# K of the first 48 units transposed on TensorE as pairs of bf16 in 4-byte elements

## The chip, the cores and the metric

One core of a Trainium2 chip. The metric is the device time of one execution in microseconds. "The profile" of a kernel is one profiled execution of it.

A word on names. The kernel works through 512 **units** (32 batches of 16 heads; 256 units belong to problem A, then 256 to problem B). One **step** of its schedule handles one unit on each engine, each engine being some units ahead of or behind the others. PE is TensorE, PEld its weight loads, DVE is VectorE, ACT is ScalarE, POOL is GpSimd.

## The reference, cut to what matters

Two independent problems with the same shapes, outputs side by side:

```python
B, Sq, D = 16, 144, 448          # x: B x Sq x D
H, Sk, Dh = 16, 512, 256         # k_cache, v_cache: B x H x Sk x Dh
q = (x @ wq).reshape(B, Sq, H, Dh).transpose(0, 2, 1, 3)
scores = einsum("bhqd,bhkd->bhqk", q, k_cache) * Dh ** -0.5
p = softmax(scores, axis=-1)
o = einsum("bhqk,bhkd->bhqd", p, v_cache)
return o.transpose(0, 2, 1, 3).reshape(B, Sq, H * Dh) @ wo
```

Everything is bf16. The scores matmuls of both kernels take K with its 256 columns d on the partitions (`lhsT` in `t_s` below), and so K has to be transposed. The scores that these inputs give are so small that a wrong K still passes the comparison with the reference. So "correct" says little about K here; that the changed kernel pairs the right columns is argued from its indices, not shown.

## The kernel before

K of units 48 to 511 is transposed by the DMA on its way in, 16 units at a time. K of the first 48 units (`P0 = 48`) is loaded as it lies, two units a load, into the same buffers as V, and is transposed on TensorE. Partition p holds keys 4p to 4p+3, 256 columns each, as one row of 1024 bf16.

```python
tr_ps = (s_ps[2][:, :].bitcast(BF16), qp_ps[:, 1, :].bitcast(BF16))   # two PSUM banks
ident = qt_sb[:, NQT - 1, 0, 0:128]                                   # bf16 identity

def t_tr(U, k):                       # half k (0, 1) of unit U; cut
    bank, eng = (("s2", DVE), ("qp1", ACT))[k]
    def e(t):
        for c in range(4):
            a = (4 * k + c) * 128
            ins = t.transpose(tr_ps[k][:, c * 128:(c + 1) * 128], v_sb[:, sl, j, a:a + 128], ident)
        return ins
    S.add(PE, e, ...)
    def ev(g):                        # eviction: DVE for half 0, ACT for half 1
        dst = kt_sb[:, 4 * k:4 * k + 4, ko:ko + 128]
        src = tr_ps[k][:, 0:512].rearrange("p (c q) -> p c q", c=4)
        ...

def t_q(U):                           # Q of one unit: 8 matmuls of 144 columns
    for dc in range(2):
        for kc in range(4):
            c0 = h * DH + dc * 128
            ins = t.matmul(acc, lhsT=wq_sb[:, kc, c0:c0 + 128], rhs=xt_sb[...], ...)

def t_s(U):                           # scores: 8 matmuls of 144 columns, in two banks
    ins = t.matmul(s_ps[bank][:, ...], lhsT=kt_sb[:, 2 * c + dc, ko:ko + 128], rhs=qt_sb[:, qsl, dc, :], ...)
```

In `t.transpose(out, in, ident)` the data are the stationary operand (the weight load), and the identity is the one that moves: 128 columns a transpose. (The records of the run with half the moving columns, below, show it: 64 rows of 128 columns as weight load 64x128, the 64x64 identity in the matmul.)

The order within one step i decides what each engine does first, because an engine takes its instructions in this order, as PE's timeline below shows from 55.13 to 57.08 us (cut to the first 48 units):

```python
t_tr(i + 4, 0)                    # PE: transposes, half 0;  DVE: K eviction
t_q(i + 3); t_evac_q(i + 3)       # PE: Q;                   DVE: Q eviction
t_s(i + 2)                        # PE: scores;              ACT: two exponentials
t_tr(i + 4, 1)                    # PE: transposes, half 1;  ACT: K eviction
t_pv(i); t_sum(i)                 # PE: P times V, sum
t_presum(i + 2)                   # POOL
t_ln(i); t_recip(i)               # ACT: reciprocal of the sum
t_check(i); t_evac_ot(i)          # DVE: two checks of the sum, output eviction
```

## Time and profile before

| | before |
|---|---|
| median of 3 runs | 1057.1 us (1055.59 to 1058.32) |
| profiled span | 1055.3 us |
| PE busy | 98% |
| units 12 to 28 (start of PV to start of PV) | 32.15 us, 2.01 us a unit |
| units 28 to 48 (output projection added) | 51.71 us |
| units 240 to 320 (change from A to B) | 171.06 us |

The stretches are from the start of one unit's first PV matmul to that of another in the profile.

The page of the kernel before: the span, the busy line, and the chain of waits by engine.

```profile
span 1055.3 us, 32320 instructions
...
PE 1031.0 (98%) x12376; PEld 875.0 (83%) x12376; DVE 740.9 (70%) x2039; ACT 793.9 (75%) x2365; POOL 636.6 (60%) x1030
...
PE 91%; DMA 5%; ACT 1%; DVE 1%; SPq 1%; issue 0%; POOL 0%; ACTq 0%; DVEq 0%
```

TensorE is busy nearly all the time, and most of the chain runs through it. "Busy" counts matmuls that overlap in the records (below, a block of eight Q matmuls is recorded as 0.66 us, and the next block starts 0.50 us after it), and so the step has to be read from starts. This is the timeline of PE in the first stage (start us, duration us, engine, line, operation, output and inputs, shape, count):

```profile
55.07 0.23 PE L1158 MATMUL ot_ps<-ps_sb,ones 128*128 128x144 bf16 x1
55.13 0.39 PE L1000 MATMUL s_ps<-qt_sb,v_sb 128*128 128x128 bf16 x4
55.35 0.66 PE L1052 MATMUL qp_ps<-xt_sb,wq_sb 128*128 128x144 bf16 x8
55.85 0.66 PE L1086 MATMUL s_ps<-qt_sb,kt_sb 128*128 128x144 bf16 x8
56.35 0.39 PE L1000 MATMUL qp_ps<-qt_sb,v_sb 128*128 128x128 bf16 x4
56.58 0.66 PE L1142 MATMUL ot_ps<-pt_sb,v_sb 128*128 128x144 bf16 x8
57.08 0.23 PE L1158 MATMUL ot_ps<-ps_sb,ones 128*128 128x144 bf16 x1
```

A block of eight Q matmuls takes 0.50 us from its start to the next block's, 62.5 ns each. Four bf16 transposes take 0.22 us, 56 ns each (the trace has starts to the nanosecond). There is no gap. From one sum matmul to the next it is 2.01 us.

Weight loads of the same stretch (20 to 110 us), by group (busy us, mean ns of one, idle before):

```profile
L1052 PEld LDWEIGHTS qp_ps<-xt_sb,wq_sb 128*128 128x128 bf16 x320 | 20.4, 98 | 0.0
L1000 PEld LDWEIGHTS s_ps<-qt_sb,v_sb 128*128 128x128 bf16 x160 | 11.3, 98 | 4.1 <-DVE run_sb L1209 1.0 <-DVE qt_sb L1065 0.7
```

PE's longest waits on loads other than those at the start (total us, times, longest us):

```profile
PE qp_ps L1052 <- DMA wq_sb<-in_B_wq_dram: 3.6, 1, 3.6
PE s_ps L1086 <- DMA kt_sb<-in_B_k_cache_dram: 2.9, 1, 2.9
```

Both stand between units 240 and 320, where problem A gives way to problem B (at 527 and at 602 us).

### The profile page before, as it was taken

The numbers are of one execution on the slowest core, as the hardware profiler recorded it, in microseconds if no ns is written. First come the engines' busy times: TensorE is split into PE (matmuls) and PEld (weight loads), VectorE is DVE, ScalarE is ACT, GpSimd is POOL, SyncE is SP. The second block draws the span as 40 slices with busy tenths as digits, with TensorE's granted clock in tenths as the row PEclk, the third lists the DMA queues.
The fourth block names the chain that finished last, engine by engine and source line by source line (L and its number), as shares of the span: only waits on it lengthen the run. The fifth ranks groups of instructions, "written<-read, shape, count | busy, mean of one in ns | idle before, by whom it ended". The sixth has DMA issues, their size and how long they took to land.

```text
span 1055.3 us, 32320 instructions
## 1 busy us (share of the span) xinstructions
PE 1031.0 (98%) x12376; PEld 875.0 (83%) x12376; DVE 740.9 (70%) x2039; ACT 793.9 (75%) x2365; POOL 636.6 (60%) x1030
## 2 busy tenths in 40 slices
PE   6999999999999999999999899999999999999997
PEld 6999888888888888888878788888888888888885
DVE  4776666776766777777868667677776667777775
ACT  4887667777777777878857667777877777788785
POOL 3554556656666566666746556566666666666673
PEclk9999999999999999999999999999999999999999
DMA  9999999999999999999999999999999999999960
GB/s 316 372 343 291 294 291 248 283 299 271 264 305 260 248 286 262 304 289 280 283 281 343 279 283 287 303 284 292 251 279 280 278 286 298 296 254 274 292 201 14
DMA packets 589060, 294.15 MB, mean 279 GB/s; under 512 B 500832, under 2 KB 513632, under 8 KB 588896
## 3 DMA queue, kind: packets, MB, share of 16 engines
q1 hardware_dynamic: 588896, 291.99, 110.9%
q8 instruction: 99, 1.62, 0.6%
q14 instruction: 65, 0.53, 0.2%
HBM read 161.48 MB, written 4.13 MB: 157 GB/s over the span
## 4 chain that ended last, share of the span: by engine, by line
PE 91%; DMA 5%; ACT 1%; DVE 1%; SPq 1%; issue 0%; POOL 0%; ACTq 0%; DVEq 0%
PE s_ps L1086 23%; PE ot_ps L1142 23%; PE qp_ps L1052 22%; PE op_ps L1259 19%; DMA kt_sb<-in_B_k_cache_dram 2%; DMA v_sb<-in_A_k_cache_dram 2%; PE ot_ps L1158 2%; PE s_ps L1000 1%; PE qp_ps L1000 1%; DMA wq_sb<-in_B_wq_dram 1%; PE qp_ps L1259 1%; ACT rinv_sb L1179 0%; ACT pt_sb L1096 0%; DVE ring L1194 0%; DVE qt_sb L1066 0%
## 5 line engine op out<-in xcount | busy, mean ns | idle before, releaser
L1106 POOL TENSOR_TENSOR pp_sb<-pt_sb 128x288 f32<-128x288 bf16 x512 | 384.9, 752 | 322.5 <-ACT pt_sb L1096 308.1
L1096 ACT ACTIVATE pt_sb<-s_ps 128x288 bf16<-128x288 f32 x1024 | 364.6, 408 | 184.4 <-PE s_ps L1086 177.6
L1194 DVE TENSOR_TENSOR ring<-ot_ps,rinv_sb 128x288 bf16<-128x288 f32 (+2 forms) x640 | 241.9, 394 | 150.3 <-ACT rinv_sb L1179 145.8
L1086 PE MATMUL s_ps<-qt_sb,kt_sb 128*128 128x144 bf16 x4096 | 341.3, 226 | 4.7 <-DMA kt_sb<-in_B_k_cache_dram 2.9
L1142 PE MATMUL ot_ps<-pt_sb,v_sb 128*128 128x144 bf16 x4096 | 340.3, 226 | 0.0
L1086 PEld LDWEIGHTS s_ps<-qt_sb,kt_sb 128*128 128x128 bf16 x4096 | 287.7, 98 | 56.9 <-DVE qt_sb L1066 5.6
L1179 ACT ACTIVATE rinv_sb<-ln_sb 64x144 f32<-64x144 f32 x928 | 298.3, 321 | 24.3
L1052 PE MATMUL qp_ps<-xt_sb,wq_sb 128*128 128x288 bf16 (+1 forms) x2368 | 302.3, 271 | 6.6 <-DMA wq_sb<-in_B_wq_dram 3.6
L1259 PE MATMUL op_ps<-wo_sb,ring 128*128 128x448 bf16 x1120 | 285.2, 353 | 0.0
L1052 PEld LDWEIGHTS qp_ps<-xt_sb,wq_sb 128*128 128x128 bf16 x2368 | 212.3, 98 | 81.9 <-issue 7.5
L1142 PEld LDWEIGHTS ot_ps<-pt_sb,v_sb 128*128 128x128 bf16 x4096 | 274.5, 98 | 0.5
L1111 POOL TENSOR_TENSOR p_sb<-pp_sb 128x144 f32<-128x144 f32 x464 | 227.5, 490 | 74.6 <-DVE ps_sb L1120 10.4
L1209 DVE TENSOR_REDUCE run_sb<-ot_ps 128x1 bf16<-128x144 f32 x560 | 146.5, 304 | 79.4 <-ACT ln_sb L1166 44.3
L1120 DVE TENSOR_TENSOR ps_sb<-p_sb 64x144 bf16<-64x144 f32 x464 | 158.7, 342 | 44.4 <-POOL p_sb L1111 30.3
L1066 DVE CAST qt_sb<-qp_ps 128x576 bf16<-128x576 f32 x216 | 162.1, 751 | 21.3 <-PE qp_ps L1052 17.7
L1259 PEld LDWEIGHTS op_ps<-wo_sb,ring 128*128 128x128 bf16 x1120 | 94.0, 98 | 21.2
L1166 ACT ACTIVATE ln_sb<-ot_ps 128x144 f32<-128x144 f32 x232 | 67.9, 293 | 32.6 <-PE ot_ps L1158 25.3
L1158 PE MATMUL ot_ps<-ps_sb,ones 128*128 128x144 bf16 x280 | 63.4, 226 | 0.0
L1065 DVE CAST qt_sb<-qp_ps 128x288 bf16<-128x288 f32 x80 | 35.9, 448 | 4.8 <-PE qp_ps L1052 4.3
L1008 ACT ACTIVATE kt_sb<-qp_ps 128x512 bf16<-128x512 bf16 x48 | 28.9, 603 | 7.3 <-PE qp_ps L1000 7.3
L1111 POOL TENSOR_TENSOR ps_sb<-pp_sb 128x144 bf16<-128x144 f32 x48 | 23.5, 490 | 6.9 <-PE ot_ps L1158 0.3
L1158 PEld LDWEIGHTS ot_ps<-ps_sb,ones 128*128 128x128 bf16 x280 | 27.5, 98 | 0.0
(29 smaller groups left out, 153.4 us busy)
## 6 DMA issues: line engine op xcount, KB each, us to landing
v_sb<-in_A_v_cache_dram SPq DMA_DIRECT2D x128, 512.0 KB, 7.1
v_sb<-in_B_v_cache_dram SPq DMA_DIRECT2D x128, 512.0 KB, 7.5
v_sb<-in_A_k_cache_dram SPq DMA_DIRECT2D x24, 512.0 KB, 9.6
out_dram<-ost_sb SPq DMA_DIRECT2D x36, 112.0 KB, 6.2
wo_sb<-in_A_wo_dram SPq DMA_DIRECT2D x8, 448.0 KB, 8.7
wo_sb<-in_B_wo_dram SPq DMA_DIRECT2D x8, 448.0 KB, 9.0
wq_sb<-in_A_wq_dram SPq DMA_DIRECT2D x4, 768.0 KB, 10.1
wq_sb<-in_B_wq_dram SPq DMA_DIRECT2D x4, 768.0 KB, 10.6
```

The source lines that it names most:

```text
L1052: ins = t.matmul(acc, lhsT=wq_sb[:, kc, c0:c0 + 128], rhs=xt_sb[:, kc, xo:xe + 1:max(xe - xo, 1), :], start=(kc == 0), stop=(kc == 3))
L1066: return v.tensor_copy(qt_sb[:, a:b + 1:b - a, :, :], qp_ps[:, :, 0:2 * SQ].rearrange("p e (u q) -> p u e q", u=2))
L1086: ins = t.matmul(s_ps[bank][:, (c % 2) * SQ:(c % 2 + 1) * SQ], lhsT=kt_sb[:, 2 * c + dc, ko:ko + 128], rhs=qt_sb[:, qsl, dc, :], start=(dc ...
L1096: return a.activation(pt_sb[:, psl, 2 * k:2 * k + 2, :].rearrange("p b q -> p (b q)"), s_ps[bank][:, 0:2 * SQ], AF.Exp, scale=DH ** -0.5)
L1106: return g.tensor_tensor(pp_sb[:, :, :], pt_sb[:, psl, 0:2, :], pt_sb[:, psl, 2:4, :], op=ALU.add)
L1111: return g.tensor_tensor(dst, pp_sb[:, 0, :], pp_sb[:, 1, :], op=ALU.add)
L1120: return v.tensor_tensor(ps_sb[p0:p0 + 64, sl, :], p2_sb[0:64, :], p2_sb[64:128, :], op=ALU.add)
L1142: ins = t.matmul(ot_ps[ob][:, dc * SQ:(dc + 1) * SQ], lhsT=v_sb[:, vsl, j, c * DH + dc * 128:c * DH + (dc + 1) * 128], rhs=pt_sb[:, sl, c, ...
L1179: return a.activation(rinv_sb[p0:p0 + 64, sl, :], ln_sb[h0:h0 + 64, :], AF.Exp, scale=-1.0)
L1194: ins = v.tensor_tensor(ring[:, 2 * h:2 * h + 2, r0:r0 + q1 - q0], ot_ps[ob][:, 0:2 * SQ].rearrange("p (c q) -> p c q", c=2)[:, :, q0:q1], ...
L1209: return v.tensor_reduce(run_sb[:, k, j:j + 1], ot_ps[ob][:, 2 * SQ:3 * SQ], axis=AX.X, op=op)
L1259: ins = t.matmul(acc[0:m, 0:D], lhsT=ring[:, c, col0:col0 + m], rhs=wo_sb[:, c, :], start=(c == first), stop=(c == last))
```

## The change

Its intent: two neighbouring bf16 are one 4-byte element. Transposed as such, half as many transposes move the same data (192 and not 384 in the profiles). A row of the result then holds, for a pair of columns d = 2j, 2j+1, both values of each key next to each other. Scores take every second bf16 of it as weights, and Q of these units must pair up in the same way, so it takes `wq` columns in steps of two.

```diff
-        tr_ps = (s_ps[2][:, :].bitcast(BF16), qp_ps[:, 1, :].bitcast(BF16))
-        ident = qt_sb[:, NQT - 1, 0, 0:128]
+        tr_ps = (s_ps[2][:, :], qp_ps[:, 1, :])
+        ident = qt_sb[:, NQT - 1, :, :].rearrange("p e q -> p (e q)").bitcast(F32)[:, 0:128]
...      (a second memset for ones of 4 bytes, from which ident is made)
+        def k_nat(U):
+            c0 = U // KW % (KR // KW) * KW * 128 + U % 2 * 1024
+            return kt_sb[:, U % KW // 2, c0:c0 + 1024]
...
-                for c in range(4):
-                    a = (4 * k + c) * 128
-                    ins = t.transpose(tr_ps[k][:, c * 128:(c + 1) * 128], v_sb[:, sl, j, a:a + 128], ident)
+                for c in range(2):
+                    a = (2 * k + c) * 256
+                    ins = t.transpose(tr_ps[k][:, c * 128:(c + 1) * 128], v_sb[:, sl, j, a:a + 256].bitcast(F32), ident)
...
-                dst = kt_sb[:, 4 * k:4 * k + 4, ko:ko + 128]
-                src = tr_ps[k][:, 0:512].rearrange("p (c q) -> p c q", c=4)
+                dst = kn[:, k * 512:(k + 1) * 512]
+                src = tr_ps[k][:, 0:256].bitcast(BF16)
...
-                        c0 = h * DH + dc * 128
+                        c0 = h * DH
+                        cols = slice(c0 + dc, c0 + DH, 2) if U < P0 else slice(c0 + dc * 128, c0 + (dc + 1) * 128)
-                        ins = t.matmul(acc, lhsT=wq_sb[:, kc, c0:c0 + 128],
+                        ins = t.matmul(acc, lhsT=wq_sb[:, kc, cols],
...
-                                           lhsT=kt_sb[:, 2 * c + dc, ko:ko + 128],
+                            lhsT = (k_nat(U)[:, c * 256 + dc:(c + 1) * 256:2] if U < P0 else
+                                    kt_sb[:, 2 * c + dc, ko:ko + 128])
```

More of the change, by code (lines that the diff above doesn't have):

```diff
@@ L852, in bass_concat_heads__mha_block_cached__gqa_block_cached__near_ridge_kernel @@
         op_ps = ps("op_ps", [128, 512], F32)
-        tr_ps = (s_ps[2][:, :].bitcast(BF16), qp_ps[:, 1, :].bitcast(BF16))
-        ident = qt_sb[:, NQT - 1, 0, 0:128]
+        tr_ps = (s_ps[2][:, :], qp_ps[:, 1, :])
+        ident = qt_sb[:, NQT - 1, :, :].rearrange("p e q -> p (e q)").bitcast(F32)[:, 0:128]
+        ones_f = pp_sb[:, :, :].rearrange("p e q -> p (e q)")[:, 0:128]
         id_key = (("qt", NQT - 1), -1)
@@ L911, in t_init, with e6 @@
             S.add(POOL, e4, writes=[("ones", 0)], name="ones")
+            def e6(g):
+                return g.memset(ones_f, 1.0)
+            S.add(POOL, e6, writes=[("pp", -1)], name="onesf")
             def e5(g):
-                return g.affine_select(ident, ones[:], pattern=[[1, 128]], compare_op=ALU.is_equal,
+                return g.affine_select(ident, ones_f, pattern=[[1, 128]], compare_op=ALU.is_equal,
                                        fill=0.0, base=0, channel_multiplier=-1)
-            S.add(POOL, e5, reads=[("ones", 0)], writes=[id_key], name="ident")
+            S.add(POOL, e5, reads=[("pp", -1)], writes=[id_key], name="ident")
         def t_load_wq(pr, hg):
@@ L986, in t_tr @@
             sl = v_seq["n", G] % NV
-            ko = U % KR * 128
             kt_key = ("kt", U // KW % (KR // KW))
@@ L994, in t_tr @@
             key = (("sp", 2), "qp1")[k]
+            kn = k_nat(U)
             def e(t):
                 ins = None
-                for c in range(4):
-                    a = (4 * k + c) * 128
-                    ins = t.transpose(tr_ps[k][:, c * 128:(c + 1) * 128], v_sb[:, sl, j, a:a + 128], ident)
+                for c in range(2):
+                    a = (2 * k + c) * 256
+                    ins = t.transpose(tr_ps[k][:, c * 128:(c + 1) * 128], v_sb[:, sl, j, a:a + 256].bitcast(F32), ident)
                 return ins
@@ L1085, in e @@
                         for dc in range(2):
-                            ins = t.matmul(s_ps[bank][:, (c % 2) * SQ:(c % 2 + 1) * SQ],
-                                           lhsT=kt_sb[:, 2 * c + dc, ko:ko + 128],
+                            lhsT = (k_nat(U)[:, c * 256 + dc:(c + 1) * 256:2] if U < P0 else
+                                    kt_sb[:, 2 * c + dc, ko:ko + 128])
+                            ins = t.matmul(s_ps[bank][:, (c % 2) * SQ:(c % 2 + 1) * SQ], lhsT=lhsT,
                                            rhs=qt_sb[:, qsl, dc, :], start=(dc == 0), stop=(dc == 1))
```

## The prediction

> **What bounds it now.** TensorE. The page's busy line has PE at 98%, and the chain of waits gives PE 91%, DMA 5%. The change touches the first 48 units (to about 112 us). The timeline shows two stretches there:
> - To about 33 us the loads set the pace: the transposes of natural K blocks 0, 1, 3, 4, 6 start 0.1 us after their block lands.
> - From 33 us on, TensorE does. Two units take 4.02 us. From start to start a 144-column matmul takes 62.5 ns and a 128-column bf16 transpose 56 ns: per unit 25 x 62.5 (8 Q, 8 S, 8 PV, 1 sum) + 8 x 56 = 2.01 us, exactly the measured step. From unit 28 on, output projection is added (2.4 us a unit).
>
> **What changes.** 384 bf16 transposes become 192 4-byte ones of the same 128 columns. The evictions stay: 96 of 128x512 bf16 (DVE 414 ns, ACT 603 ns), only the destination becomes contiguous. 768 weight loads (K and wq of 48 units) read every second bf16. One small memset is added on POOL before the first K block lands at 4.5 us: free. The order on PE, DVE, ACT and SP stays.
>
> **Cost of the new pieces.**
> 1. A 4-byte transpose. [...] The trace of before has no 4-byte matmul. I take 56 to 65 ns; a unit then saves 4 x 56 = 224 ns. If its weight load is slow[...], it may be 110 ns, saving nothing; in four passes, 225 ns, costing 0.45 us a unit.
> 2. Strided weight loads. [...] Weight loads in the trace start as little as 15 to 17 ns apart where nothing holds them, so even three times slower they hide under the 62.5 ns matmul.
>
> **How much is on the path.** Not the first 12 units (loads). About 36 units: 36 x 0.224 = 8.1 us. Can the rest follow 3.57 us for two units? Loads: between 33 and 62 us K blocks land every 3.3 us with V and wo between them, so yes, but their lead (5 to 7 us by 60 us) grows to 2 or 3 us only. ACT: about 1.7 us a unit by busy time, less from start to start; close but fits. The first K by transposing DMA (issued 94 us, landed 115.6, needed 119.1) moves earlier with the units before it; its 3.5 us lead shrinks to about 2. After that TensorE paces everything, and it shifts along. I take off about 1 us for new short waits.
>
> **Prediction: 1050 us**, 8 in 10 between 1046 and 1060. Faster by over 2%: 0.02; within 2%: 0.94; slower by over 2%: 0.04.
>
> **Right or wrong in the profile.** Right: new transposes start 56 to 65 ns apart; Q and S matmuls stay at 62.5 ns; two units take about 3.6 us between 35 and 70 us; unit 48's scores start near 111 us, not 119; later stages unchanged. Wrong: transposes at about 110 (time unchanged) or 225 ns (about 1073 us); Q or S of these units over 63 ns; new PE waits for natural K or V before 70 us, or for the first transposing K load.
>
> **What would make it wrong.** Mostly the 4-byte pass rate; next, the stride making weight loads longer than a matmul; last, loads that can't keep up.

## More of the kernel before

Busy time by stretch (us from the start: length, busy us and count of PE, PEld, DVE, ACT and POOL, granted clock, DMA share, GB/s):

```profile
34.00:74.00 40.00, 40.00 (x660) 40.00 (x658) 30.71 (x98) 34.04 (x100) 23.90 (x39) 1.00 1.07 356
...
504.00:544.00 40.00, 36.42 (x455) 31.51 (x453) 28.67 (x71) 28.83 (x87) 24.10 (x39) 0.96 1.17 291
```

In the first of these PE is full. Between 504 and 544 us it is not, and its clock was granted at 0.96 on average.

## The result, and the profile after

| | before | after |
|---|---|---|
| median of 4 runs each | 1056.34 us (1055.59 to 1058.32) | 1059.51 us (1058.27 to 1060.47) |
| profiled span | 1055.3 us | 1058.7 us |
| from start to start of a transpose, first stage | 56 ns, eight a unit | 109 ns, four a unit |
| units 12 to 28 | 32.15 us | 32.15 us |
| units 28 to 48 | 51.71 us | 51.57 us |
| start of unit 240 | 506.9 us | 505.8 us |
| units 240 to 320 | 171.06 us | 176.28 us |

The ratio is 1.0023, with a 95% interval of 1.0004 to 1.0042: slower by less than the 2% that would count, but clear of the noise. A ratio is the mean time of one kernel's fast runs over that of the other's of the same rounds, so not quite the ratio of the medians.

The page after:

```profile
span 1058.7 us, 31937 instructions
...
PE 1032.0 (97%) x12184; PEld 874.0 (83%) x12184; DVE 745.1 (70%) x2039; ACT 793.4 (75%) x2365; POOL 634.7 (60%) x1031
...
PE 92%; DMA 5%; ACT 1%; DVE 1%; issue 0%; SPq 0%; ACTq 0%; DVEq 0%
```

The timeline of PE in the first stage of the changed kernel, over the same part of a step:

```profile
54.27 0.23 PE L1169 MATMUL ot_ps<-ps_sb,ones 128*128 128x144 bf16 x1
54.34 0.38 PE L1009 MATMUL s_ps<-qt_sb,v_sb 128*128 128x128 f32 x2
54.55 0.67 PE L1062 MATMUL qp_ps<-xt_sb,wq_sb 128*128 128x144 bf16 x8
55.06 0.66 PE L1098 MATMUL s_ps<-qt_sb,kt_sb 128*128 128x144 bf16 x8
55.56 0.38 PE L1009 MATMUL qp_ps<-qt_sb,v_sb 128*128 128x128 f32 x2
55.78 0.66 PE L1153 MATMUL ot_ps<-pt_sb,v_sb 128*128 128x144 bf16 x8
56.28 0.23 PE L1169 MATMUL ot_ps<-ps_sb,ones 128*128 128x144 bf16 x1
```

Two 4-byte transposes take 0.21 to 0.22 us up to the next block's start, as long as four bf16 ones did. The blocks of Q and scores are 0.50 us as before (0.51 where Q follows a transpose), although every weight load in them now skips every second element.

The weight loads after, same stretch and columns as before:

```profile
L1062 PEld LDWEIGHTS qp_ps<-xt_sb,wq_sb 128*128 128x128 bf16 x320 | 21.1, 98 | 1.7
L1009 PEld LDWEIGHTS s_ps<-qt_sb,v_sb 128*128 128x128 f32 x80 | 9.2, 141 | 3.5 <-DVE run_sb L1220 1.2 <-DVE qt_sb L1075 0.4
```

A 4-byte weight load is recorded as 141 ns and not 98. The strided one of wq stays at 98 ns.

PE's waits at the change from A to B, and busy time by stretch:

```profile
PE qp_ps L1062 <- DMA wq_sb<-in_B_wq_dram: 7.1, 1, 7.1
...
PE s_ps L1098 <- DMA kt_sb<-in_B_k_cache_dram: 3.6, 1, 3.6
```

```profile
34.00:74.00 40.00, 40.00 (x581) 38.44 (x579) 31.06 (x100) 33.98 (x101) 24.38 (x40) 1.00 1.08 357
...
504.00:544.00 40.00, 32.95 (x397) 28.18 (x395) 25.94 (x62) 25.73 (x77) 20.76 (x35) 0.87 1.17 276
```

This is where the 3.4 us between the two profiles come from. Up to unit 240 the changed kernel is 1.1 us ahead: about 0.8 us from first loads that landed sooner, 0.14 us from units 28 to 48, 0.16 us from units 48 to 240. Then it loses 5.2 us to unit 320, and gets 0.7 us back to the end: -1.1 + 5.2 - 0.7 = 3.4. The wait for the first weights of B is 7.1 us and not 3.6. The records of the clock show half speed for 10.2 us in one piece from 528.0 us on, within that wait, which ended at 532.6; in the kernel before it was 3.4 us, from 530.9, with the wait over at 530.2. In that piece a block of eight scores matmuls took 0.96 us (from 531.37) and not 0.50.

Each of the two kernels has a second piece at half speed after its wait for B's K: 3.4 us long in both, from 606.0 us and from 609.9. What starts such a piece and what sets its length is not shown: a wait of 2.5 us was followed by one in one run (the kernel before with another order on DVE, below), and a wait of 3.4 us by none in another (half the moving columns).

So there were two questions. Why does a 4-byte transpose take 109 ns? And what of the rest of the sum: would 8 us have come if it had taken 55?

### The profile page after: what moved, and what is told of

Its sections match the earlier page's. It is cut to its first block, busy times and chain, and to the rows that moved or that the text cites. A ratio compares the mean times of both kernels' runs of the same rounds, so it can differ in the third digit from the quotient of the medians.

```text
span 1058.7 us, 31937 instructions
## 1 busy us (share of the span) xinstructions
PE 1032.0 (97%) x12184; PEld 874.0 (83%) x12184; DVE 745.1 (70%) x2039; ACT 793.4 (75%) x2365; POOL 634.7 (60%) x1031
## 4 chain that ended last, share of the span: by engine, by line
PE 92%; DMA 5%; ACT 1%; DVE 1%; issue 0%; SPq 0%; ACTq 0%; DVEq 0%
PE s_ps L1098 23%; PE ot_ps L1153 23%; PE qp_ps L1062 23%; PE op_ps L1270 19%; DMA kt_sb<-in_B_k_cache_dram 2%; PE ot_ps L1169 2%; DMA v_sb<-in_A_k_cache_dram 1%; PE s_ps L1009 1%; PE qp_ps L1009 1%; DMA wq_sb<-in_B_wq_dram 1%; PE qp_ps L1270 1%; ACT rinv_sb L1190 1%; DMA xt_sb<-in_A_x_dram 0%; ACT pt_sb L1107 0%; DVE qt_sb L1076 0%
## 5 line engine op out<-in xcount | busy, mean ns | idle before, releaser
L1131 DVE TENSOR_TENSOR ps_sb<-p_sb 64x144 bf16<-64x144 f32 x464 | 161.1, 347 | 38.1 <-POOL p_sb L1122 23.5
```

Source lines behind the costliest of these rows:

```text
L1131: return v.tensor_tensor(ps_sb[p0:p0 + 64, sl, :], p2_sb[0:64, :], p2_sb[64:128, :], op=ALU.add)
```

## The experiments

Runs were made in five calls; each call went to another chip and has its own timed runs of the kernel before on it. Stretches come from one profile each, so a stretch is often set against a profile from another chip.

### What sets the 109 ns: the moving side or the weight load

In the trace of before, bf16 matmuls of 144 columns start 62.5 ns apart and transposes of 128 columns 55.8 (the 56 ns of above). My estimate from these two: 0.42 ns a column and 2.5 ns a matmul. At twice the time a column, 128 columns would take 109 ns, and that is what was measured. But a weight load of 128 columns might be the limit as well. So: half the moving columns behind the same weight load, twice.

```diff
-                    ins = t.transpose(tr_ps[k][:, c * 128:(c + 1) * 128], v_sb[:, sl, j, a:a + 256].bitcast(F32), ident)
+                    for m in (0, 64):
+                        ins = t.transpose(tr_ps[k][:, c * 128 + m:c * 128 + m + 64],
+                                          v_sb[0:64, sl, j, a:a + 256].bitcast(F32), ident[0:64, 0:64])
```

> Wrong result on purpose. Each 4-byte transpose of 128 moving columns is replaced by two of 64 moving columns (64 rows by 64 identity) behind the same 128-column weight load. Theory H1, the moving identity of 4-byte elements streams at half rate [...]: each half-size transpose starts about 55 to 60 ns after the last, so a block of four takes about as long as the two did (about 220 ns). Rival H2, the 4-byte weight load (142 ns long against 98 ns) sets the pace: each half-size transpose still starts about 109 ns after the last, a block takes 437 ns, and units of the first stage take about 2.4 us and not 2.01.

Measured (one look): 1079.99 us, against a median of 1058.24 us of the kernel before in that call. PE's timeline, scores, transposes, PV:

```profile
60.38 0.66 PE L1100 MATMUL s_ps<-qt_sb,kt_sb 128*128 128x144 bf16 x8
60.97 0.46 PE L1010 MATMUL qp_ps<-qt_sb,v_sb 64*128 64x64 f32 x4
61.36 0.68 PE L1155 MATMUL ot_ps<-pt_sb,v_sb 128*128 128x144 bf16 x8
```

A block of four is 0.39 us, longer than the 0.22 expected, and 0.59 us, not 0.50, pass from the scores' start to it. In the nanoseconds of one such block, the four transposes start at 60971, 61082, 61145 and 61206: after the first, 63 and 61 ns apart. The rest is around the block: 157 ns from the last scores matmul to the first transpose (62.5 is usual), 111 ns to the second, 156 ns from the last to PV. These instructions are recorded as 64*128 and their neighbours as 128*128; the 157 and 156 ns stand where the one form changes to the other. This change of form is what the text below calls a change of tiling.

Half the columns took 61 to 63 ns in place of 109, behind a weight load of as many columns (138 ns long against 141), but of half the rows. The changed kernel's own trace settles it without half rows or a change of tiling. Its weight loads of the transposes after the scores:

```profile
55.50 0.20 PEld L1009 LDWEIGHTS qp_ps<-qt_sb,v_sb 128*128 128x128 f32 x2
```

These two loads of all 128 rows start 62 ns apart. And PV, whose own weight load is bf16, still starts 109 ns after the last transpose. So the weight load isn't what holds 109 ns. H2 falls. The moving identity of 4-byte elements holds it, at half the columns per ns (128 in 109 ns, against 128 bf16 columns in 56). (Half the columns at that rate, with the 2.5 ns per matmul, would be 56 ns by the estimate above; why it is 61 to 63 isn't settled.) My expectation of the block's length was wrong, because it left out the gaps around it, 157 and 156 ns.

### The same operands as an ordinary matmul

Without transpose mode, and with the identity as the moving operand:

```diff
-                    ins = t.transpose(tr_ps[k][:, c * 128:(c + 1) * 128], v_sb[:, sl, j, a:a + 256].bitcast(F32), ident)
+                    ins = t.matmul(tr_ps[k][:, c * 128:(c + 1) * 128], lhsT=v_sb[:, sl, j, a:a + 256].bitcast(F32),
+                                   rhs=ident, start=True, stop=True)
```

> The same 4-byte operands as an ordinary matmul with the identity and no transpose mode[...]. [...] If transpose mode is a single pass at half rate and the ordinary matmul is four such passes: about 4 x 109 = 437 ns from start to start. If an ordinary 4-byte matmul is four passes at full rate: about 215 to 225 ns, and transpose mode gains only two times. If mode makes no difference: 109 ns.

Measured (one look): 1077.62 us. PE's timeline:

```profile
60.49 0.66 PE L1009 MATMUL qp_ps<-qt_sb,v_sb 128*128 128x128 f32 x4
60.98 0.66 PE L1155 MATMUL ot_ps<-pt_sb,v_sb 128*128 128x144 bf16 x8
```

The program has two ordinary matmuls in this block; the trace shows four. The second starts 157 ns after the first, and from then on they start 111 to 113 ns apart (0.49 us for the block). So an ordinary 4-byte matmul of 128 columns is recorded as two of 111 to 113 ns, some 223 ns in all, and a 4-byte transpose as one of 109. Transpose mode gains two times here. The 225 ns of my prediction, an estimate of four times the 56 ns of a bf16 transpose, are about what the ordinary matmul takes; that a transpose would take only 56 to 65 of them was a guess that no trace showed, and it was wrong. (That a matmul is made of passes isn't shown either: the trace has two records of 111 to 113 ns.)

### Is the stride free

bf16 transposes as before, but of every second column of K, with wq in steps of two; right result.

```diff
-                    a = (4 * k + c) * 128
-                    ins = t.transpose(tr_ps[k][:, c * 128:(c + 1) * 128], v_sb[:, sl, j, a:a + 128], ident)
+                    a = (2 * k + c // 2) * 256 + c % 2
+                    ins = t.transpose(tr_ps[k][:, c * 128:(c + 1) * 128], v_sb[:, sl, j, a:a + 255:2], ident)
...      (wq columns as in the change)
```

> The stride without the 4-byte elements: bf16 transposes that take every second column of K, with wq in steps of two; right result. Theory (stride is free): transposes 56 ns, Q 62.5 ns, two units in 4.02 us, time within 3 us of the kernel before. Rival (stride costs): transposes or Q over their former intervals and the first stage longer than 112 us.

Measured: 1056.07 us, ratio 0.9985 (0.9963 to 1.0007). Transposes 56 ns, Q 62.5 ns, units 12 to 28 in 32.15 us, 28 to 48 in 51.71 us: to the hundredth the kernel before. The stride is free here.

### If a transpose had cost what I predicted

From unit 4 on, one of the two 4-byte transposes of each half is left out: 2 x 109 = 219 ns a unit, which is what I had predicted for four of 55. Its output is wrong, which doesn't matter for the time.

```diff
-                for c in range(2):
+                for c in range(2 if U < 4 else 1):
```

> Wrong result on purpose: from unit 4 on, only one of the two 4-byte transposes of each half is done, so a unit has 2 x 109 = 219 ns of transposes, just what I had predicted for four of 55 ns. If the rest of my sum holds, 36 units save 0.23 us each: two units in about 3.57 us, unit 48 some 8 us sooner, 1047 to 1051 us in all (ratio 0.991 to 0.995). If the loads of the first stage can't follow, two units stay above 3.7 us and a PE wait for natural K or V shows before 70 us. If the load-bound stretch after unit 240 takes it back, unit 240 comes 8 us sooner but the total gains less than 5 us.

The same with bf16: two of the four transposes of each half.

```diff
-                for c in range(4):
+                for c in range(4 if U < 4 else 2):
```

> Wrong result on purpose: the same saving with bf16 transposes (two of four in each half from unit 4 on, 2 x 112 = 224 ns a unit). Theory: as the run with half of the 4-byte ones within 2 us, 1047 to 1051 us. If 4-byte transposes make the stretch after unit 240 slower by themselves, this run is 3 us or more below the other.

| | before | half, 4-byte | half, bf16 |
|---|---|---|---|
| median | 1057.52 us | 1050.48 us | 1054.33 us |
| ratio | | 0.9941 (0.9923 to 0.9958) | 0.9967 (0.995 to 0.9984) |
| units 12 to 28 | 32.15 us | 32.15 us | 32.17 us |
| units 28 to 48 | 51.71 us | 48.89 us | 48.59 us |
| units 240 to 320 | 171.06 us | 168.39 us | 173.2 us |

(The stretches of the kernel before are those of its profile above.) In units 28 to 44 it works: 38.46 and 38.51 us in place of 41.63, about 0.20 us a unit. Units 44 to 48 have nothing to save, because transposes run four units ahead; and there the 4-byte half run lost 0.35 us, as PE waited 0.7 us for the first transposing K load. In units 12 to 28 a saving of 0.22 us a unit is worth nothing at all, in both. So two expectations failed: two units took 4.02 us and not 3.57, and the medians of the two runs lie 3.9 us apart and not within 2. The last row favours the 4-byte kernel, so 4-byte transposes don't make that stretch slow by themselves.

So TensorE wasn't the only limit of the first stage. These are PE's waits of the half run between 34 and 74 us; the kernel before shows none in that stretch:

```profile
PEld qp_ps L1062 <- DVE qt_sb L1075: 2.3, 10, 0.2
PEld s_ps L1009 <- DVE kt_sb L1017: 1.7, 10, 0.2
```

Small waits, for DVE's evictions of Q and of K. The timeline of the half run over two units shows what DVE is late for (lines of other engines left out):

```profile
50.20 0.71 ACT L1107 ACTIVATE pt_sb<-s_ps 128x288 bf16<-128x288 f32 x2 [0.45 <-PE s_ps L1098]
...
50.80 0.60 ACT L1017 ACTIVATE kt_sb<-qp_ps 128x512 bf16<-128x512 bf16 x1
...
51.07 0.67 PE L1062 MATMUL qp_ps<-xt_sb,wq_sb 128*128 128x144 bf16 x8
51.28 0.31 ACT L1177 ACTIVATE rinv_sb<-ot_ps 128x144 f32<-128x144 f32 x1
...
51.62 0.53 DVE L1220 TENSOR_REDUCE run_sb<-ot_ps 128x1 bf16<-128x144 f32 x2 [0.61 <-ACT rinv_sb L1177]
...
52.06 0.45 DVE L1205 TENSOR_TENSOR ring<-ot_ps,rinv_sb 128x288 bf16<-128x288 f32 x1
...
52.42 0.42 DVE L1017 COPY kt_sb<-s_ps 128x512 bf16<-128x512 bf16 x1
...
52.75 0.45 DVE L1075 CAST qt_sb<-qp_ps 128x288 bf16<-128x288 f32 x1
...
53.26 0.49 PEld L1062 LDWEIGHTS qp_ps<-xt_sb,wq_sb 128*128 128x128 bf16 x8 [0.23 <-DVE qt_sb L1075]
53.26 0.68 PE L1062 MATMUL qp_ps<-xt_sb,wq_sb 128*128 128x144 bf16 x8
...
53.77 0.66 PE L1098 MATMUL s_ps<-qt_sb,kt_sb 128*128 128x144 bf16 x8
...
54.22 0.71 ACT L1107 ACTIVATE pt_sb<-s_ps 128x288 bf16<-128x288 f32 x2 [0.46 <-PE s_ps L1098]
```

Follow it from 50.20 us. ACT's two exponentials are followed by its K eviction (50.80) and, behind that, the logarithm of the sum (51.28). DVE waits for it (0.61 us), does the checks (51.62) and the output eviction (52.06), and only then the next K eviction (52.42) and the Q eviction (52.75). The Q in question had been done since 51.74. PE's next Q waits for that eviction (53.26), scores follow (53.77), and ACT's next exponentials have waited for them (54.22). From 50.20 to 54.22 is 4.02 us, for two units. There is no K transpose in this chain. In the kernel before, TensorE's own work for two units, 50 x 62.5 + 16 x 56 ns, is 4.02 us as well: two limits of the same length.

To test that, the checks and the output eviction are moved on DVE behind the next step's K and Q evictions (first 48 units only). In the half run:

```diff
                     t_q(u)
                     t_evac_q(u)
+            if 0 < i <= P0:
+                t_check(i - 1)
+                t_evac_ot(i - 1)
...
                     t_recip(u)
-                    t_check(u)
-                t_evac_ot(u)
+                if u >= P0:
+                    if u % 2 == 0:
+                        t_check(u)
+                    t_evac_ot(u)
```

> The half run with 4-byte transposes (wrong result on purpose), and the two checks and the output eviction of each of the first 48 units moved on DVE behind the next step's K and Q evictions. Theory L: in units 12 to 28 a second chain as long as TensorE's own work holds the step at 4.02 us (scores, exponentials and K eviction on ACT, reciprocal, checks and output eviction on DVE, then the K and Q evictions queued behind them, then the next Q), so the half run gained nothing there; with Q's eviction no longer behind the output's, two units fall to 3.6 to 3.75 us, units 12 to 28 from 32.15 to 29 to 30 us. Rival D (loads hold 4.02 us): no change, 32.1 us. Rival A (ACT alone, about 1.7 us a unit busy): 3.9 us or more.

And in the kernel before, as the control:

> The kernel before with that order on DVE; right result. There TensorE alone needs 25 x 62.5 + 8 x 56 ns a unit, 4.02 us for two, so if TensorE and the second chain are equal limits, units 12 to 28 stay at 32.1 us within 0.1 and the time within 2 us of the kernel before. Shorter than 31.9 us would mean that the count of TensorE's work is wrong.

| | half, 4-byte | the same, DVE order changed | before, DVE order changed |
|---|---|---|---|
| ratio to before | 0.9941 | 0.9916 (0.9892 to 0.994) | 1.001 (0.9985 to 1.0035) |
| median | 1050.48 us | 1048.61 us | 1057.17 us |
| units 12 to 28 | 32.15 us | 28.51 us | 32.15 us |
| units 28 to 48 | 48.89 us | 49.70 us | 51.71 us |
| first scores of unit 48 | 116.2 us | 111.8 us | |

The order alone takes 3.6 us out of units 12 to 28 of the half run, and nothing out of those of the kernel before, where TensorE holds the same 32.15 us by itself. 28.51 us for 16 units is 1.78 us a unit, exactly 25 x 62.5 + 219 ns; now TensorE alone holds it. Loads were the same in both runs, so neither loads nor ACT by itself were the limit: rivals D and A fall. With both corrections the total gains the 8 us of the prediction (1048.61 us against 1057.05 of the kernel before), but part of them elsewhere than predicted. This profile ends 8.4 us sooner than that of the kernel before: 1.8 us come from before unit 12, where the prediction counted nothing (and where six profiles of kernels with all their bf16 transposes differ by 1.2 us, so part of it may be chance), 3.6 from units 12 to 28, 2.0 from units 28 to 48 and 1.0 from the rest. In units 28 to 44 it gained 3.2 us, and from 44 to 48 it lost 1.2 again, in this wait:

```profile
PE s_ps L1098 <- DMA kt_sb<-in_A_k_cache_dram: 1.5, 1, 1.5
```

The first transposing K load landed at 111.6 us, and the scores of unit 48 began 0.14 us later; in the kernel before they came 3.5 us after the landing. So the next limit stood close behind the second one.

### Two row halves at once

The blocks above suggested something. A transpose of 64 rows moves only 64 columns of identity (64x64 in the records), and its starts were 61 to 63 ns apart. If the two row halves of a transpose, which lie on partitions 0 to 63 and 64 to 127, ran at once, two would take the time of one; that they can was a guess until this run. Half 0 goes to one bank and half 1 to the other (both in one bank was not measured):

```diff
-                for c in range(2):
-                    a = (2 * k + c) * 256
-                    ins = t.transpose(tr_ps[k][:, c * 128:(c + 1) * 128], v_sb[:, sl, j, a:a + 256].bitcast(F32), ident)
+                for c in range(4):
+                    for kk in range(2):
+                        m = kk * 64
+                        ins = t.transpose(tr_ps[kk][:, c * 64:(c + 1) * 64],
+                                          v_sb[m:m + 64, sl, j, c * 256:(c + 1) * 256].bitcast(F32),
+                                          ident[m:m + 64, m:m + 64])
...      (one block a unit; evictions write the two key halves; right result)
```

> 4-byte transposes of 64 rows each[...]; right result. If they run at once and weight loads don't bind: eight in about 4 x 55 = 220 ns plus some cost of changing the tiling, against 437 ns for four full ones; two units in about 3.6 to 3.8 us. If they run one after the other, or the eight weight loads bind: 440 ns or more, two units in 4.0 to 4.2 us, time the same or a little longer than after.

Measured: 1060.96 us, ratio 1.0037 (1.0009 to 1.0064). PE's timeline: the sum, the first two pairs of transposes, and (after the cut) the last transpose and Q:

```profile
60.76 0.23 PE L1173 MATMUL ot_ps<-ps_sb,ones 128*128 128x144 bf16 x1
60.91 0.27 PE L1010 MATMUL s_ps<-qt_sb,v_sb 64*128 64x64 f32 x1
60.92 0.27 PE L1010 MATMUL qp_ps<-qt_sb,v_sb 64*128 64x64 f32 x1
61.03 0.22 PE L1010 MATMUL s_ps<-qt_sb,v_sb 64*128 64x64 f32 x1
61.03 0.22 PE L1010 MATMUL qp_ps<-qt_sb,v_sb 64*128 64x64 f32 x1
...
61.15 0.22 PE L1010 MATMUL qp_ps<-qt_sb,v_sb 64*128 64x64 f32 x1
61.31 0.68 PE L1066 MATMUL qp_ps<-xt_sb,wq_sb 128*128 128x144 bf16 x8
```

The pairs run at once: each pair's second starts 3 ns after its first, and pairs follow one another every 57 to 62 ns after the first 111. But the block needs 157 ns to get in and 154 out, so that from sum to Q it takes 0.55 us, against 0.50 us for the sum and the four whole transposes of a unit (62.5 + 4 x 109 ns). What the concurrency gains, the changes of tiling cost: 157 and 154 ns where a bf16 matmul of 144 columns takes 62.5.

Pay that once for two units, then:

```diff
+                for jj in range(2):
                     for c in range(4):
                         for kk in range(2):      # columns jj * 256 + c * 64 of the bank
...      (a block at even units only; each unit's evictions stay in its own step)
```

> Row halves at once, as in the run of the row tiles, but for two units in one block, so that the change of tiling is paid once for two units. From that run's intervals (157 ns into the block, 111 for the first pair, 61 to 62 for each later pair, 157 out of it): 157 + 111 + 6 x 61 + 157 = 791 ns for two units, of which 62 belong to the sum matmul: 729 ns against 8 x 109 = 872 in the changed kernel and 16 x 56 = 896 in the kernel before. Two units in about 3.85 us and not 4.02, stage one about 3 us shorter by unit 48. The total may hide it, since the stretch after unit 240 varies by more. If the evictions in a burst hold up the row halves, two units stay at 4.0 us or more.

Measured: 1055.26 us, ratio 1.0001 (0.9988 to 1.0014). Units 12 to 28 took 33.07 us, longer than before, and 28 to 48 took 50.24 us, 1.5 us less. In the first stretch PE waited ahead of the block for ACT. Evictions of both units directly after the block:

> Row halves for two units in one block, with both units' evictions directly after the block. In the run before it, the second unit's eviction by ACT came late and PE waited for it ahead of the block: two units took 4.07 us between 42 and 58 us. If that wait was all that kept the block's gain away, two units take 3.8 to 3.9 us here, and unit 48 comes 2 to 3 us sooner than in the kernel before. If ACT then delays the exponentials, or the loads bind, 3.95 us or more.

Measured: 1054.41 us, ratio 0.9972 (0.9956 to 0.9988), units 12 to 28 in 32.53 us. Half of a us better, but far from 3.85 us for two units; the late eviction wasn't all. The order on DVE, tried on it as well:

> The row halves for two units with early evictions (ratio 0.997 in the last call), and that order on DVE; right result. TensorE's count for two units is 50 x 62.5 + 729 = 3.85 us. Theory L: units 12 to 28 fall from 32.5 to 30.8 to 31.2 us, two units 3.85 to 3.9 us, and unit 48 another 1.3 us sooner; time 1051 to 1055 us, the best of all if the stretch after unit 240 doesn't take it back. Otherwise 32 us or more, and the time of the last call.

Measured: units 12 to 28 in 31.0 us, two units in 3.87 us, as expected; first scores of unit 48 at 115.5 us against 119.1. The profiled span is 1047.9 us, the shortest with a right result. But its timed runs give 1054.51 us and 0.998 (0.9955 to 1.0006). So the 4-byte transpose can be made to gain in its own stage, by both lessons together, and what reaches the end is about 0.3% at best: the kernel with the early evictions beat the kernel before by that, clear of the noise, in one call; the last can't be told from it. The changed kernel itself was slower than the kernel before in both comparisons.

### Where the 2 to 3 us between the kernels come from

Both kernels again, unchanged:

> The kernel before, unchanged, as a control. Theory R (the 0.2% is real and sits at the boundary between the problems): ratio 1.000 within 0.001, and in its trace the wait of PE for the B weights near 526 us is again about 3.6 us. Rival N (that wait varies from run to run whatever the kernel): the wait differs from 3.6 us by 2 us or more, or the ratio strays as far as 1.002.

> The changed kernel, unchanged, as a control. Theory R: ratio again 1.002 to 1.003 and a wait of about 7 us for the B weights. Rival N: ratio anywhere from 0.998 to 1.003 with the wait following it.

The kernel before: 1057.96 us, ratio to itself 1.0013 (0.9987 to 1.0038). That is the noise. Wait for B's weights 4.8 us, units 240 to 320 in 171.9 us. The changed kernel: 1060.76 us, ratio 1.0035 (1.0011 to 1.0059), wait 7.9 us, units 240 to 320 in 175.9 us. So both the difference and its place came back; rival N falls.

That wait's load stands behind the first transposing K load of B. With the order of the two turned round (a load of V, v127, moved ahead with it):

```diff
-    MID = ("k16 v127 v128 q0 v129 ...
+    MID = ("v127 q0 k16 v128 v129 ...
...      (the list still starts where k16 was due)
```

> The kernel before, with the first load of B weights issued ahead of the first transposing K load of B and not behind it. If the wait for these weights comes from standing behind that K load, it vanishes (before: 3.6 us, and the clock of TensorE falls after it), K then lands at about 531 us and may be waited for by up to 2 us: time 1 to 4 us less than before.

> The same reordering on the changed kernel. If its 2.4 us over the kernel before sit in that wait alone, this run equals the reordered kernel before within 1 us, or beats it by up to 1 us (unit 48 starts 0.9 us sooner). If they come from elsewhere, it stays 2 to 3 us above.

| | ratio to before | wait for B's weights | longest wait for B's K | units 240 to 320 |
|---|---|---|---|---|
| before, reordered | 1.0026 (1.0001 to 1.0051) | 3.1 us | 4.5 us | 173.1 us |
| after, reordered | 1.0001 (0.9978 to 1.0024) | 1.3 us | 3.0 us | 174.8 us |

In the timed runs this order left no excess of the changed kernel (1.0001 against 1.0026, where the unchanged two gave 1.0035 and 1.0013). But my expectation of a gain failed: the waits moved, to K and (after, reordered) to V, 3.1 us, and the stretch got no shorter than the best of the kernel before. So it isn't one load in the wrong place; the loads as a whole hold this stretch. From the issue of the first K of B to the landing of the third, the DMA engines had no idle moment in either kernel's trace, and the same orders took 104.5 us in the kernel before and 109.7 us after. Over all twenty profiles the stretch goes with these loads (correlation 0.92): from the start of unit 240 to the landing of B's third K load it was 94.9 us where the stretch took 168.2, 97.9 at 171.1 (before) and 103.1 at 176.3 (after). Which drives the other this doesn't say. The slow clock doesn't decide it: the kernel with the 168.2 us, the first with two units in one block, had 6.8 us of it after its first wait, and the kernel before 3.4.

Does the shift of 1 us decide how they fall? Idle transposes were added at unit 40:

```diff
-                for c in range(2):
+                for c in list(range(2)) * (5 if (U, k) == (40, 1) else 1):     # 9 for sixteen; in the kernel before likewise
```

> The changed kernel with eight transposes of unit 40 repeated (8 x 109 ns = 0.87 us of idle work, result unchanged), so that unit 240 starts near 506.7 us as in the kernel before, not at 505.7. Theory T (the changed kernel's 4 to 5 us between units 240 and 320 come from how its loads happen to fall in time there, which a shift of a microsecond alters): the stretch from unit 240 to 320 falls from 176 us to between 169 and 174, time at or below that of the kernel before plus 1 us. Rival P (it belongs to the changed program whatever the shift): 175 us or more again, ratio about 1.003 to 1.004.

> The same with sixteen repeats (1.75 us). Theory T: the stretch takes anything from 169 to 176 us, not in proportion to the delay. Rival P: 175 us or more, and the time is 0.9 us over that of the eight repeats.

> The kernel before with sixteen bf16 transposes of unit 40 repeated (16 x 56 ns = 0.9 us). Theory T: the stretch from unit 240 to 320 may leave the 171 to 172 us that it took twice, in either direction. Rival P: 171 to 172 us again, time 0.9 us above the kernel before.

| | ratio to before | start of unit 240 | units 240 to 320 | start of unit 320 |
|---|---|---|---|---|
| after | 1.0023 | 505.8 us | 176.3 us | 682.1 us |
| after, +0.87 us | 1.0035 (1.0022 to 1.0048) | 506.7 us | 174.4 us | 681.1 us |
| after, +1.75 us | 1.0024 (1.0011 to 1.0037) | 507.7 us | 173.3 us | 681.0 us |
| before | | 506.9 us | 171.1 us | 678.0 us |
| before, +0.9 us | 1.0044 (1.0023 to 1.0065) | 507.1 us | 172.4 us | 679.5 us |

Neither theory holds as I put it. In the changed kernel the added work cost nothing: unit 320 starts no later, the delay is absorbed in the stretch. In the kernel before 0.9 us of added work cost about 4.6 us (0.44%; interval 2.4 to 6.9) in the timed runs (six, from 1055.7 to 1063.6), of which its one profile shows only 1. Over all profiles, this stretch took 168.8 to 173.2 us in kernels with bf16 transposes and 168.2 to 176.3 us in kernels with 4-byte ones. So what is shown is the place (loads at the change of problem), and that the stretch varies by several us between programs whose other parts are alike, in a way that comes back in a second run of the same program. Why the changed program's loads fall badly stays open.

## Why the prediction was wrong, point by point

- **The step that failed**: "A 4-byte transpose. ... I take 56 to 65 ns." It measured 109 ns. The term of the sum, 36 units x 0.224 us = 8.1 us, then is 36 x (8 x 56 - 4 x 109) ns = 0.4 us. The alternative was in the text ("it may be 110 ns, saving nothing"), but for the wrong reason: I put it to the weight load, and the run with half the moving columns (61 to 63 ns), with the changed kernel's own trace (weight loads 62 ns apart), shows the moving side. (110 and 225 were estimates too, about two and four times the 56 ns of a bf16 transpose.) The third case of the text, 225 ns, did not come.
- **"From 33 us on, TensorE does"** was half of it. The count (25 x 62.5 + 8 x 56 = 2.01 us) was right, and it hid a second chain of the same 4.02 us for two units through ACT, DVE and PE. "ACT ... close but fits" looked at busy time, where each engine by itself has room, and not at the order in which DVE serves TensorE. Even at 55 ns, units 12 to 28 would have gained nothing. Shown by the half runs and by the order on DVE.
- **Strided weight loads hide**: right. Q and scores stayed at 62.5 ns, and bf16 transposes with a stride at 56.
- **Loads can follow in the first stage**: right for natural K and V as far as tested. The half run with the new order on DVE went at 1.78 us a unit without a PE wait on loads in units 12 to 28. For the first transposing K load it was wrong: "its 3.5 us lead shrinks to about 2", but in that run PE waited 1.5 us for it.
- **"After that TensorE paces everything, and it shifts along"** was wrong at the change of problem. There loads pace it, the stretch took 5.2 us longer, and nearly all the difference between the kernels lies in it. I had seen the waits there (3.6 and 2.9 us) in the profile of before and not counted them as a place where time can go.
- **1050 us, 1046 to 1060**: the measured 1059.51 us lies inside the range, but that is no support: the gain that it was centred on did not come. The low chance of anything over 2% was right.

## What to carry to other kernels

Before counting on fewer, wider instructions, find or measure the rate of the wider ones; half as many at half the rate is the same time (here 4 x 109 ns for 8 x 56). When an engine shows no gap, ask what the next limit is and how far away: take some of its work out, even with a wrong result, and see whether the step gets shorter. And where loads hold a stretch, a microsecond saved ahead of it, or the run of another program through it, may come out as anything within several us (here 168.2 to 176.3 us for the stretch); read the stages apart before explaining a total.
